# A state-space convolution block with a gated feed-forward on one core: ScalarE's table sets named in the program at four places of the front and once behind the last exponents

## The chip, the core and the metric

The kernel runs on one core of a Trainium2 chip, as one program. The metric is the device time of one execution in microseconds (us); lower is better. The core has TensorE (matrix products), VectorE and GpSimd (elementwise work), ScalarE (elementwise functions by table), and SyncE, which here only issues transfers. Each has a queue of its own that is worked off in order, and semaphores order one against another. In the views they are called PE (and PEld for its weight loads), DVE, POOL, ACT and SP.

## The reference

`x` is 2048 x 640, the state size is 128, the hidden size of the feed-forward 1728, all float32.

```python
mod = (silu(c) @ w_mod).reshape(1, 6, 1, 640)       # shift, scale, gate, twice
h = layernorm(x) * (1 + ca) + sa
x = x + ga * A(h)
h = layernorm(x) * (1 + cb) + sb
x = x + gb * B(h)

def A(u):                                           # a long convolution per channel
    dt = exp(log_dt)[:, None]
    logdA = dt * (A_re + 1j * A_im)
    P = exp(logdA[:, :, None] * arange(2048))
    K = einsum("dn,dnl,dn->dl", C, P, dt * B).real   # 640 filters of length 2048
    return irfft(rfft(u, 4096) * rfft(K, 4096))[:2048] + u * Dskip

def B(x):
    return (silu(x @ w1) * (x @ w3)) @ w2
```

## The kernel before

The program has three stretches: a front, a stretch in an order written out by hand (`ROUND`), and the feed-forward.

**The filters.** The powers `P` are built in polar form. `polar(cs, E)` (L237) works on the columns `cs` of the channels and turns `B` times `C` into a logarithm of its size (Square, then `Ln`, L256), an angle (`Abs`, `Arctan`, L262, and two `Sign`, L263 and L264), and the phases of the powers as integers (`thi`, `phi`). It is a generator: the program calls it once for channels 0 to 127 (`first`, on VectorE) and once for channels 128 to 639 (`rest`, whose first products are GpSimd's), in three steps each, with other work between the steps. Then, by blocks of 16 channels numbered 0 to 39, `exps` multiplies the logarithms by the powers' exponents on TensorE (`exp_fast`, L432, and `exp_slow`, L444, into the banks `pa` and `pq`) and takes the exponential on ScalarE (`fast`, `slow`: the tables `A`). `phases` forms the phase table `ph` on GpSimd, `absph`, `cosine` and `sine` take its absolute value, cosine and sine on ScalarE, and `real1`, `real2`, `imag1`, `imag2` (L497 to L508) multiply size by phase on VectorE into `E` and `A`. `kgen` (L521), `k1evac` and `k_stage1` (L539) make of these the filters and the first half of their Fourier transform; `k_out` copies it into `uk`.

**The input.** `ln1_load` brings tiles `x` of 128 rows, seven at a time, `ln1_norm` takes two of them through the layernorm (VectorE's statistics L377, GpSimd's power, VectorE's L381, ScalarE's Identity), and `u_stage1` (L406) does the first half of their transform: TensorE into `pu`, ScalarE's copy or VectorE's sums (L411, L412) into `u`, SyncE's store to `us` (L413).

**The modulation.** `mod_early`, `mod_shift`, `mod_gate` and `mod_cols` multiply silu(c) by `w_mod` on TensorE (L299, L310, L324, L333, L343) between the rest, with VectorE's copies `part` (L301). The silu of `c` itself is made of an exponential and a reciprocal.

**The front's loop** runs `tk` from 0 to 9. In the rounds `tk` = 2 and 6 it calls `exps` twice, for four blocks; after the second pair of round 2 it takes a step of `rest` (`next(rest)`), which holds `Ln`, `Arctan` and `Sign`; then come cosine and sine of the next block. ScalarE's instructions of the front are held in the program's order (`act`, L135, and `acopy`, L138, pass each to `keep_in_program_order`). VectorE's, TensorE's, GpSimd's and SyncE's are ordered by a scheduler there.

**ROUND** (10 rounds of 4 blocks) is one list of steps that all engines but SyncE follow: the rest of the filters, and by `stage2` (L570), `k_copy` (the copy `kc`), `products`, `sums`, `inverse1` (L612) and `z_store` the second half of the transforms, the product and the inverse, into `zs`. The tail of the convolution, `tk` from 41, has no exponents any more; at its first step the tables' room is given back (`tabs.close()`).

**The feed-forward** takes half of the tokens at a time and runs under L102, where a helper records every operation. It uses `Silu`, copies, casts and Identity of ScalarE.

**Table sets.** ScalarE's functions lie in tables, several functions to a set, and a set has to be loaded (`ACT_TABLE_LOAD`) before a function of it runs. The program before names none; the loads are put in when it is built, each ahead of the first function that the loaded set lacks.

Of the kernel before, what the change touches and what calls it, by code (L numbers as in the profile page):

```python
# [107 lines left out]
def tile_kernel(ctx: ExitStack, tc: tile.TileContext, a):  # L108
    nc = tc.nc
    V, S, G, PE = nc.vector, nc.scalar, nc.gpsimd, nc.tensor  # L110
# [22 lines left out]
    def act(*args, **kw):  # L133

        return tc.keep_in_program_order(S.activation(*args, **kw))  # L135

    def acopy(out, in_):
        return tc.keep_in_program_order(S.copy(out, in_))  # L138

    def ln_stats(pool, x):  # L140
        st = pool.tile([P, 2, 6], F32, name="st")
        V.bn_stats(st[:, 0, :], x[:, :320])
        V.bn_stats(st[:, 1, :], x[:, 320:])
        mv = pool.tile([P, 2], F32, name="mv")
        V.bn_aggr(mv, st)
        rs = pool.tile([P, 2], F32, name="rs")
        G.tensor_tensor(rs[:, 0:1], mv[:, 1:2], epst[:, 0:1], op=OP.add)
        G.tensor_tensor(rs[:, 1:2], rs[:, 0:1], epst[:, 1:2], op=OP.pow)
        return mv[:, 0:1], rs[:, 1:2]
# [87 lines left out]
    def polar(cs, E):  # L237

        are, aim, br, bi, cr, ci = (prm[:, i, cs] for i in range(6))
        ld, dtc, m, t, g_r, g_i = (v[:, cs] for v in (ldt, dt, m0, t3, gr, gi))  # L240
        k0, nk = cs.start // P, (cs.stop - cs.start) // P

        E.tensor_tensor(g_r, br, cr, op=OP.mult)
        E.tensor_tensor(m, bi, ci, op=OP.mult)
        E.tensor_tensor(g_r, g_r, m, op=OP.subtract)
        V.tensor_tensor(g_i, br, ci, op=OP.mult)
        V.tensor_tensor(t, bi, cr, op=OP.mult)
        V.tensor_tensor(g_i, g_i, t, op=OP.add)
        q, q2, ag, ai = br, bi, cr, ci
        act(q, g_r, AF.Square)  # L250
        act(q2, g_i, AF.Square)
        act(ag, g_r, AF.Abs)
        act(ai, g_i, AF.Abs)
        yield
        V.scalar_tensor_tensor(q, q, 1e-36, q2, op0=OP.max, op1=OP.add)
        act(q, q, AF.Ln)  # L256

        V.tensor_tensor(m, ag, ai, op=OP.subtract)
        V.scalar_tensor_tensor(t, ag, 1e-30, ai, op0=OP.max, op1=OP.add)
        V.reciprocal(q2, t)  # L260
        V.tensor_tensor(m, m, q2, op=OP.mult)
        act(m, m, AF.Arctan)  # L262
        act(ag, g_r, AF.Sign, scale=-1.0)  # L263
        act(ai, g_i, AF.Sign, scale=-1.0, bias=tiny)  # L264

        V.scalar_tensor_tensor(aim, aim, 0.25 / math.pi, dtc, op0=OP.mult, op1=OP.mult)
        magic = 12582912.0
        V.tensor_scalar(t, aim, magic, None, op0=OP.add)
        V.tensor_scalar(t, t, -magic, None, op0=OP.add)
        V.tensor_tensor(aim, aim, t, op=OP.subtract)  # L270
        V.tensor_scalar(thi[:, cs], aim, TURN, 2147483520.0, op0=OP.mult, op1=OP.min)
        yield

        nat = lambda v: v.rearrange("n (k p r j) -> n k r p j", k=nk, p=4, r=4)
        rows = lambda v: v[:, :nk * P].rearrange("n (k r p j) -> n k r p j", k=nk, p=4, r=4)
        for k in range(nk):
            E.tensor_tensor(rows(lt[:, 0])[:, k], nat(are)[:, k], nat(dtc)[:, k], op=OP.mult)
        for k in range(nk):
            V.tensor_tensor(rows(lt[:, 1])[:, k], nat(q)[:, k], nat(ld)[:, k], op=OP.add)
        for i, (hi, lo) in enumerate(((lah, lal), (lmh, lml))):  # L280
            pT = psS.tile([P, 2, 512], F32, name="pT", tag="AB"[i], bufs=1)
            for k in range(nk):
                PE.transpose(pT[:, 0, k * P:(k + 1) * P], lt[:, i, k * P:(k + 1) * P], ident)
            pv = pT[:, 0, :nk * P].rearrange("p (k n) -> p k n", k=nk)
            acopy(hi[:, k0:k0 + nk], pv)
            V.tensor_tensor(lo[:, k0:k0 + nk], pv, hi[:, k0:k0 + nk].bitcast(F32), op=OP.subtract)

        V.tensor_scalar(m, m, 0.5 / math.pi, 0.125, op0=OP.mult, op1=OP.add)
        V.tensor_tensor(m, m, ag, op=OP.mult)
        V.scalar_tensor_tensor(m, m, 0.25, ai, op0=OP.add, op1=OP.mult)  # L290
        V.tensor_scalar(phi[:, cs], m, TURN, 2147483520.0, op0=OP.mult, op1=OP.min)
# [132 lines left out]
    def exp_fast(steps):  # L424

        for s in steps:
            pA[s] = psS.tile([P, 2, 512], F32, name="pa", tag="AB"[s % 2] if not in_order[0] else "B", bufs=1)
        for w, st in ((lah, True), (lal, False)):
            for s in steps:
                ch, js, rows = exp_rows(s)  # L430
                for rr, r in rows:
                    keep(PE.matmul(pA[s][:, rr, :], w[r, ch, :], r2[r, js, :].rearrange("p j b -> p (j b)"),  # L432
                                   start=st, stop=not st, tile_position=(r.start, 0)))
# [13 lines left out]
    def fast(s):  # L447

        AA[s] = a_table()
        act(AA[s][:, :, 0:3:2, :], pA.pop(s).rearrange("p r (j h b) -> p (r j) h b", j=8, h=2), AF.Exp)  # L450
# [5 lines left out]
    def exps(s, between=()):  # L456

        steps = (s, s + 1)
        exp_fast(steps)
        for i in steps:  # L460
            fast(i)
        for fn in between:
            fn()
        exp_slow(steps)
        for i in steps:
            slow(i)
# [247 lines left out]
    def do(name, k):  # L714
# [4 lines left out]
        done.add((name, k))  # L719
        return (conv if name in conv else parts)[name](k)  # L720

    act(sc, cT, AF.Exp, scale=-1.0)
    act(dt, ldt, AF.Exp)
    V.tensor_scalar(sc, sc, 1.0, None, op0=OP.add)
# [22 lines left out]
        ln1_load(j)  # L747
    nc.sync.dma_start(prm[:, :, d1], prma[:, :, d1])
    mod_shift()
    exps(0)  # L750
    ln1_norm(0)
    exps(2)
# [21 lines left out]
    for tk in range(LAG):  # L774
        if tk == SPC + 1:
            mod_cols(4, wm[4])
            pre.close()
            fp = ssm.enter_context(tc.tile_pool(name="fp", bufs=2, side="right", reuse_waits="tile"))

        def transform_k():  # L780
            if 0 <= tk - 1:
                do("kg", tk - 1)
            if 0 <= tk - 2:
                do("pt", tk - 2)
                do("uk", tk - 2)

        do("PH", tk + 3)
        do("AB", tk + 2)
        if tk % EB == EB - 2:
            exps(tk + 2)  # L790
            transform_k()
            exps(tk + 4)
            done.update((n, k) for n in ("PA", "XA", "PQ", "XQ") for k in range(tk + 6))
            if tk == 2:
                next(rest)
        do("CO", tk + 2)
        do("SI", tk + 2)
        if tk % EB != EB - 2:
            transform_k()
        for n in ("E1", "E2", "A1", "A2"):  # L800
            do(n, tk)
        if 0 <= tk - 1:
            do("K", tk - 1)
        if tk < 6:
            for j in (2 * tk + 4, 2 * tk + 5):
                u_stage1(j)
            for j in (2 * tk + 7, 2 * tk + 8):
                if j < NT:
                    ln1_load(j)
            if tk + 3 < 8:  # L810
                ln1_norm(tk + 3)
        if tk == 0:
            next(rest)
        if tk == 3:
            next(rest, None)
            wm = []
        if 4 <= tk < 9:
            wm.append(w_load(w_room(2, tk % 2, WC, 2048), 1920 + (tk - 4) * WC))
        if 5 <= tk < 9:
            mod_cols(tk - 5, wm[tk - 5])  # L820
        if tk == 7:
            for i in range(4):
                u_load(0, i)
# [10 lines left out]
    for rnd in range(NS // EB):  # L834
        for word in ROUND:
            name, k = word[:2].rstrip("+-"), EB * rnd + int(word[len(word[:2].rstrip("+-")):])
# [9 lines left out]
    for tk in range(NS + 1, LAG + 8 * NDC + 2):  # L846
        do("st", tk)
        do("kc", tk)
        last = do("iv", tk - 1)
        do("zt", tk - 1)  # L850
        do("T", tk)
        do("Y", tk)
        if tk == NS + 1:
            tabs.close()
            xp = ctx.enter_context(tc.tile_pool(name="xp", bufs=2))
            idle = xp.tile([P, 512], F32R, name="idle", bufs=1)
            G.memset(idle.bitcast(F32), 0.0)
            for j in range(4):
                early[j] = (x_tile(), early[j][1], xp.tile([P, KD, 6], F32, name="st5", bufs=4))
        i = tk - 1 - LAG - 8 * NDC + 8  # L860
        if 0 <= i < 8:
            if i < 4:
                z_load(early[i][1], i, (3,), q=nc.gpsimd)
            for j in ((), (), (), (), (0,), (1,), (), (2, 3))[i]:
                x_part(j, last)
# [18 lines left out]
    V, S, G, PE = (InOrder(tc, e, (in_order,)) for e in (V, S, G, PE))  # L884
# [638 lines left out]
```

## Time and profile before

| | |
|---|---|
| three runs | 984.60, 984.23, 985.72 us, median 984.6 |
| profiled execution, span from first to last instruction | 984.1 us (the page gives no other time of it) |
| busy: TensorE | 918.2 us, 93% |
| VectorE | 700.8 us, 71% |
| ScalarE | 541.1 us, 55% |
| GpSimd | 265.3 us, 27% |
| mean granted clock of TensorE | 0.947 of full speed |

The page's second part cuts the span into 40 slices of 24.6 us and gives each engine's busy tenths in them, and the granted clock. The timeline lists an engine's instructions: start, us, engine, line, operation, output <- input, count, and in brackets the idle time before it with what ended it. Its start is that of the instruction, which may overlap the one before by some 0.1 us. The chain of waits follows the work that ended last back from the end, at each step to what released it. The view by groups adds up instructions of one line and one shape: busy us, mean ns of one, idle us before them and its releasers.

### The profile page before, as it was taken

The numbers are of one execution on the slowest core, as the hardware profiler recorded it, in microseconds if no ns is written. First come the engines' busy times: TensorE is split into PE (matmuls) and PEld (weight loads), VectorE is DVE, ScalarE is ACT, GpSimd is POOL, SyncE is SP. The second block draws the span as 40 slices with busy tenths as digits, with TensorE's granted clock in tenths as the row PEclk, the third lists the DMA queues.
The fourth block names the chain that finished last, engine by engine and source line by source line (L and its number), as shares of the span: only waits on it lengthen the run. The fifth ranks groups of instructions, "written<-read, shape, count | busy, mean of one in ns | idle before, by whom it ended". The sixth has DMA issues, their size and how long they took to land.

```text
span 984.1 us, 20582 instructions
## 1 busy us (share of the span) xinstructions
PE 918.2 (93%) x8214; PEld 687.2 (70%) x8214; DVE 700.8 (71%) x1253; ACT 541.1 (55%) x793; POOL 265.3 (27%) x274
## 2 busy tenths in 40 slices
PE   5898797989888898789999999999999999999998
PEld 2445354766666676567888888777888888888886
DVE  4598856888988886667766665568796766654575
ACT  3667665899999983246433332355753333323432
POOL 1453333444444440214422220111152222200000
PEclk9855767999999999989999999999999999999999
DMA  9463576554665587767212311896432221113443
GB/s 267 159 228 110 220 186 186 158 131 134 159 159 154 153 219 200 252 170 259 82 55 62 99 54 52 221 281 208 135 93 67 81 68 54 54 41 90 151 148 120
DMA packets 103572, 140.74 MB, mean 143 GB/s; under 512 B 20565, under 2 KB 62677, under 8 KB 103477
## 3 DMA queue, kind: packets, MB, share of 16 engines
q1 hardware_dynamic: 99668, 129.34, 45.5%
q0 software_dynamic: 2304, 7.74, 2.4%
q10 hardware_dynamic: 1504, 2.36, 0.9%
q8 instruction: 64, 1.05, 0.4%
q14 instruction: 32, 0.25, 0.1%
HBM read 107.94 MB, written 31.46 MB: 142 GB/s over the span
## 4 chain that ended last, share of the span: by engine, by line
PE 68%; ACT 15%; DVE 7%; DMA 4%; issue 3%; POOL 2%; SPq 1%; ACTq 0%; DVEq 0%; POOLq 0%
PE ps L102 52%; ACT cs L135 4%; ACT A L135 3%; ACT ph L135 3%; PE pa L432 2%; PE p L570 2%; ACT L135 2%; DMA zs<-zt 2%; PE pq L444 2%; PE pt L539 1%; PE pk L521 1%; PE pm L299 1%; DMA A<-zs 1%; PE pu L406 1%; PE pz L612 1%
## 5 line engine op out<-in xcount | busy, mean ns | idle before, releaser
L102 DVE TENSOR_TENSOR s<-ps,s 128x512 f32<-128x512 f32 x138 | 94.8, 687 | 79.8 <-PE ps L102 79.5
L472 POOL TENSOR_TENSOR ph<-thi,iota 128x1024 int32<-128x1024 int32 x40 | 85.4, 2135 | 175.1 <-DVE A L508 78.2
L102 DVE TENSOR_TENSOR gl<-rw,gh 128x640 fp32r<-128x640 f32 x87 | 78.1, 897 | 65.3 <-ACT gh L102 65.2
L102 ACT CAST gh<-rw 128x640 fp32r<-128x640 f32 x87 | 63.3, 727 | 103.9 <-PE ps L102 60.6
L570 PE MATMUL p<-uk,s 128*64 128x256 f32 x640 | 79.0, 389 | 13.3 <-PE pa L432 5.6
L102 PE MATMUL ps<-xA,gh 128*128 128x512 f32 x280 | 87.9, 392 | 0.4 <-ACT xA L102 0.4
L102 PE MATMUL ps<-gh,uh 128*128 128x512 f32 x224 | 87.5, 390 | 0.0
L102 PE MATMUL ps<-gl,uh 128*128 128x512 f32 x224 | 87.2, 389 | 0.0
L102 POOL TENSOR_TENSOR S<-rw 128x256 f32<-128x256 f32 x46 | 36.7, 799 | 174.0 <-DVE S0l L102 163.1
L102 PE MATMUL ps<-gh,ul 128*128 128x512 f32 x208 | 81.1, 390 | 0.0
L570 PEld LDWEIGHTS p<-uk,s 128*64 128x64 f32 x640 | 45.2, 138 | 38.5 <-PE pa L432 8.4
L102 PEld LDWEIGHTS ps<-xA,gh 128*128 128x128 f32 x280 | 52.1, 188 | 13.0 <-ACT xA L102 1.0
L102 PE MATMUL ps<-xA,gl 128*128 128x512 f32 x140 | 54.5, 390 | 0.0
L135 ACT ACTIVATE A<-pa 128x1024 f32<-128x1024 f32 x40 | 40.4, 1023 | 25.7 <-PE pa L432 24.3
L497 DVE TENSOR_TENSOR E<-A,cs 128x1024 f32<-128x1024 f32 x40 | 51.0, 1275 | 1.7 <-PE pk L521 1.7
L504 DVE TENSOR_TENSOR A<-A,ph 128x1024 f32<-128x1024 f32 x40 | 50.1, 1253 | 0.0
L612 PE MATMUL pz<-Y,i 64*128 64x128 f32 x640 | 45.2, 286 | 5.0 <-issue 3.1
L612 PEld LDWEIGHTS pz<-Y,i 64*128 64x128 f32 x640 | 39.1, 190 | 14.9 <-issue 11.4
L102 PEld LDWEIGHTS ps<-gl,uh 128*128 128x128 f32 x224 | 42.1, 188 | 8.9
L102 PEld LDWEIGHTS ps<-gh,uh 128*128 128x128 f32 x224 | 42.0, 188 | 8.8
L521 PE MATMUL pk<-E 128*32 128x64 f32 x1280 | 46.6, 232 | 1.2 <-DVE E L500 0.6
L539 PE MATMUL pt<-s,K 128*64 128x128 f32 x640 | 47.2, 291 | 0.5 <-ACT uk L138 0.5
(261 smaller groups left out, 2306.7 us busy)
## 6 DMA issues: line engine op xcount, KB each, us to landing
rw<-in_w_dram SPq DMA_DIRECT2D x52, 320.0 KB
us<-u SPq DMA_DIRECT2D x16, 640.0 KB
s<-in_s_dram SPq DMA_DIRECT2D x40, 256.0 KB
i<-in_i_dram SPq DMA_DIRECT2D x40, 256.0 KB
rw<-in_wg_dram SPq DMA_DIRECT2D x31, 320.0 KB
rw<-in_wu_dram SPq DMA_DIRECT2D x28, 320.0 KB
uk<-us SPq DMA_DIRECT2D x32, 256.0 KB
zs<-zt SPq DMA_DIRECT2D x32, 256.0 KB
```

The costliest lines, as they stand in the source:

```text
L102: ins = fn(*args, **kw)
L135: return tc.keep_in_program_order(S.activation(*args, **kw))
L299: PE.matmul(pm[g, :n], scb[:, k], w[:, k, :], start=(k < 4), stop=(k > 0), tile_position=(0, g.start))
L432: keep(PE.matmul(pA[s][:, rr, :], w[r, ch, :], r2[r, js, :].rearrange("p j b -> p (j b)"), start=st, stop=not st, tile_position=(r.start, 0)))
L444: keep(PE.matmul(pQ[s][:, rr, :256], w[r, ch, :], rv, start=(i == 0), stop=(i == 3), tile_position=(r.start, 0)))
L472: hold(G.tensor_tensor(p, bc(thi[:, sl], 2, NPH), bc(iota, 1, SD), op=OP.mult))
L497: keep(V.tensor_tensor(EC[s][:, :, 1:3, :], AA[s][:, :, 1:3, :], mid(cs[s]), op=OP.mult))
L504: keep(V.tensor_tensor(A[:, :, 1:3, :], A[:, :, 1:3, :], mid(ph[s]), op=OP.mult))
L521: keep(PE.matmul(pk[dq * 32:dq * 32 + 32, g, :], x[:, g * 4 + dq, 1, :], x[:, g * 4 + dq, 0:3:2, :], start=(st == 0), stop=(st == 1), tile ...
L539: keep(PE.matmul(pt[c * 64:c * 64 + 64, g, :], kk[:, g, :], s1[:, c, :], start=True, stop=True, tile_position=(0, c * 64)))
L570: keep(PE.matmul(p2[par * 64:par * 64 + 64, pi, c, :], s2[:, pi * 2 + par, c * 64:c * 64 + 64], uk[:, 0:kn + 1:kn, f, :], start=True, stop ...
L612: ins = keep(PE.matmul(pz[:, par, (g % 2) * 2 + pi, :], i1[r, pi, c, :], Y[r, pi, c, :], start=(c == 0), stop=(c == 1), tile_position=(par ...
```

## The change

A helper names a set, and is called at five places of the code. Since `polar` runs twice and one place is inside the loop's rounds 2 and 6, the calls come to seven.

- In `polar`, ahead of the arctangent, the set `trig_and_small`, which holds arctangent, sign, absolute value and sine.
- Ahead of the first exponentials (of `c` and `log_dt`), ahead of `exps(0)`, and ahead of `exps` in the rounds 2 and 6, the set `natural_log_exp_and_others`, which holds exponential and logarithm.
- At the first step of the convolution's tail, the set `silu_and_others`.

The named loads are held in the program's order, as ScalarE's other instructions of the front are. Where a function's set isn't there, loads are still put in when the program is built.

```diff
     def acopy(out, in_):
         return tc.keep_in_program_order(S.copy(out, in_))
+
+    def act_set(name):
+        tc.keep_in_program_order(S.preload_act_table_set(name))
...
         V.reciprocal(q2, t)
         V.tensor_tensor(m, m, q2, op=OP.mult)
+        act_set("trig_and_small")
         act(m, m, AF.Arctan)
...
+    act_set("natural_log_exp_and_others")
     act(sc, cT, AF.Exp, scale=-1.0)
     act(dt, ldt, AF.Exp)
...
     mod_shift()
+    act_set("natural_log_exp_and_others")
     exps(0)
     ln1_norm(0)
     exps(2)
...
         if tk % EB == EB - 2:
+            act_set("natural_log_exp_and_others")
             exps(tk + 2)
             transform_k()
             exps(tk + 4)
...
         if tk == NS + 1:
+            act_set("silu_and_others")
             tabs.close()
```

## The prediction

> **What bounds the kernel now.** I read the page first, then ScalarE's groups, then the chain of waits and the timelines around the places that the change touches.
>
> ```profile
> span 984.1 us, 20582 instructions
> PE   5898797989888898789999999999999999999998
> PEclk9855767999999999989999999999999999999999
> PE 68%; ACT 15%; DVE 7%; DMA 4%; issue 3%; POOL 2%; SPq 1%; ACTq 0%; DVEq 0%; POOLq 0%
> L135 ACT ACT_TABLE_LOAD x25 | 32.1, 1283 | 1.6 <-PEq L1512 1.2
> L102 ACT ACT_TABLE_LOAD x1 | 1.3, 1283 | 0.0
> ```
>
> The page gives a span and no other time of this execution: 984.1 us, 0.5 below the median of the three runs, 984.6 (984.23 to 985.72). I work on the span and move the median by the same amount. A measurement of this kernel can tell a difference of about 0.2%, 2 us, from none. TensorE carries 68% of the chain that ended last, and from slice 8 on (each is 24.6 us) it is nearly always busy at nearly full clock. The first seven slices are another kernel: TensorE less filled, and its granted clock down to half. ScalarE has 15% of the chain, and there are 26 loads of a table set, 1.283 us each. What a removed load is worth is read where it stands.
>
> **What the change does to the loads.** Placed by themselves before, each load stands where the function changes. The built program of after has 23 loads, all others in the same places of ScalarE's queue, and no load waits for a semaphore. Three go: the one ahead of the first polar part's logarithm (exponential and logarithm are now of one set), the one ahead of the logarithm of the second polar part, and the one ahead of the cosine behind the second polar part's signs (arctangent and sine are now of one set). The load for SiLU moves from the first SiLU to the tail of the convolution. ScalarE's other instructions keep their order. I cost these four one by one.
>
> First polar part, ScalarE's timeline:
>
> ```profile
> 10.05 1.28 ACT L135 ACT_TABLE_LOAD   x1
> 11.93 0.31 ACT L135 ACTIVATE uk<-uk 128x128 f32<-128x128 f32 x1 [0.60 <-DVE uk L255]
> 25.34 1.02 ACT L135 ACTIVATE A<-pa 128x1024 f32<-128x1024 f32 x1 [9.19 <-PE pa L432]
> ```
>
> The load at 10.05 ends at 11.33 and the logarithm starts at 11.93, because VectorE's L255 comes last, 0.60 later. Taking the load away moves nothing: cost zero, the cover is VectorE. The first exponents at 25.34 waited 9.19 for TensorE, so even without that cover the 1.28 would end in this wait.
>
> The trace of this place weighs a rule. The Trainium skill, "ScalarE: Activation LUTs", section "What ACT_TABLE_LOAD costs", counts 2.66 us for a switch, a load and a drain of 1.38. By the row the logarithm started 1.88 after the load did, so 2.66 does not fit here; by the rule the two loads of the second polar part would be worth 5.3 us on ScalarE, which VectorE's limit below would hold to the same sum.
>
> Second polar part, the chain of waits (start, us, what; the last row is a store of `u` that prices rival 3):
>
> ```profile
> 89.18 0.60 ACT A L135
> 89.80 1.28 ACT L135
> 91.09 0.63 ACT uk L135
> 91.74 1.28 ACT L135
> 93.57 1.23 ACT uk L135 x2
> 94.81 1.28 ACT L135
> 96.11 1.15 ACT cs L135
> 98.20 0.58 ACT u L138
> ...
> 117.00 5.44 DMA us<-u
> ```
>
> Here all three loads are on the chain. The first (89.80) and the third (94.81) go, the second stays. From the end of the last exponent, 89.18 + 0.60 = 89.78, to the logarithm at 91.09 are 1.31; from the load's start at 94.81 to the cosine at 96.11 are 1.30. ScalarE therefore stands 2.6 us earlier when it copies `u` at 98.20. I take 2.6.
>
> How much of this gets through is read from who waits behind it:
>
> ```profile
> 97.38 0.88 DVE L377 BATCH_NORM_STATS2 st<-x 128x6 f32<-128x320 f32 x2
> 98.83 2.17 PE L406 MATMUL pu<-x,misc 32*64 32x320 f32 x16 [3.73 <-ACT u L138]
> 100.25 0.82 DVE L411 TENSOR_TENSOR u<-pu,shift 128x640 f32<-128x640 f32 x1 [1.99 <-PE pu L406]
> 109.37 0.69 DVE L286 TENSOR_TENSOR lml<-pT,lmh 128x512 fp32r<-128x512 f32 x1 [0.48 <-ACT lmh L138]
> 119.23 1.73 ACT L135 ACTIVATE x<-x,rs 128x640 f32<-128x640 f32 x2 [5.74 <-DVE rs L381]
> 167.28 0.58 ACT L138 COPY kc<-p 128x512 f32<-128x512 f32 x1 [8.41 <-PE p L570]
> ```
>
> TensorE sat 3.73 for the copy and can take the whole 2.6. VectorE had waited 1.99 for TensorE at 100.25: that is all it can gain there, its own work ends at 98.26. It waits for ScalarE once more, 0.48 at 109.37, and that wait too is behind the removed loads. Together 2.47. At 119.23 ScalarE itself waits 5.74 for VectorE, so what passes this place is VectorE's gain, 2.47, not ScalarE's 2.6. Behind it the work goes on in chains of TensorE, VectorE and SyncE's stores to the first product copy at 167.28, where the order written out by hand begins. That order is the same in both programs, so a shift there reaches the end. This term: -2.5, between 0 and -2.6.
>
> SiLU's load, ScalarE's timeline at the new and at the old place:
>
> ```profile
> 383.89 0.90 ACT L694 COPY xm<-xe 128x128 f32<-128x128 f32 x4
> 386.10 0.58 ACT L138 COPY kc<-p 128x512 f32<-128x512 f32 x1 [1.31 <-PE p L570]
> 440.18 1.28 ACT L102 ACT_TABLE_LOAD   x1
> 441.91 0.60 ACT L102 ACTIVATE s<-ps 128x512 f32<-128x512 f32 x1 [0.45 <-PE ps L102]
> ```
>
> At the old place the first SiLU waited another 0.45 for TensorE, so the load was covered and removing it gains nothing. The new place is right ahead of the four small copies at 383.89. Queued behind it are these and the copy at 386.10, which waited 1.31 for TensorE; 1.28 fits into it, with 0.03 left. Cost 0, at worst 1.28 if TensorE comes that much earlier there.
>
> **The order of the other engines.** The named loads are seen by the scheduler, which sets TensorE, VectorE and SyncE anew up to about 140 us. The two built programs differ in it, and GpSimd's order does not. Three differences count.
>
> ```profile
> 18.61 0.79 PE L432 MATMUL pa<-r,lah 32*128 32x512 f32 x1
> 28.17 0.79 PE L432 MATMUL pa<-r,lal 32*128 32x512 f32 x2
> 48.08 0.61 PE L310 MATMUL pm<-misc,part 128*128 128x1 f32 x4 [1.10 <-DVE part L301]
> 43.00 0.34 SPq L368 DMA_DIRECT2D x<-in_x_dram  x1
> 55.19 0.33 SPq L413 DMA_DIRECT2D us<-u  x1
> 58.78 0.88 DVE L377 BATCH_NORM_STATS2 st<-x 128x6 f32<-128x320 f32 x2
> ```
>
> One: the first eight exponent products stood in five groups, from 18.61 to 28.17, each of 0.79 whether it held one product or two side by side on different rows of the array. In after they stand in three groups, ahead of most modulation products: at best 2 x 0.79 = 1.6 less. Two: the copy of `part` for the row at 48.08 stands ahead of a wait on GpSimd instead of behind it, at best 1.10. Both are TensorE time at a place where it is dense, yet the modulation chain that it also feeds ends where it did, so I take little: -0.5, between 0 and -2.7 (1.6 + 1.10). Three, a loss: SyncE now issues two stores of `u` ahead of the load of the eighth `x` tile, which was issued at 43.00 and now stands behind the store at 55.19. Its statistics ran at 58.78. I price it at 0, with a bound worked out as a rival below.
>
> Sum: 0 - 2.5 + 0 - 0.5 + 0 = -3.0. Forecast: 984.1 - 3.0 = 981.1 of span, 981.6 as a median.
>
> **The rivals.** (1) The clock, the slower side. The granted clock goes up and down in the front, by stages:
>
> ```profile
> 60.00:63.00 3.00, 3.00 (x48) 1.55 (x44) 2.81 (x5) 2.97 (x4) 0.51 (x2) 0.50 0.71 229
> 96.00:99.00 3.00, 0.17 (x4) 0.17 (x8) 2.25 (x6) 2.99 (x5) 2.84 (x2) 0.87 0.89 254
> 107.00:117.00 10.00, 8.13 (x210) 5.51 (x210) 9.52 (x19) 5.29 (x7) 2.95 (x2) 0.93 0.62 219
> 128.00:141.00 13.00, 12.89 (x118) 7.73 (x122) 5.04 (x9) 5.50 (x8) 4.77 (x3) 0.57 0.88 207
> ```
>
> (Columns: stage, its us, then busy of TensorE, weight loads, VectorE, ScalarE, GpSimd, then clock, DMA share, GB/s.) Moving matmuls by some us moves which of them run at which clock. If the stage from 107 to 117 lost its 0.93 and ran at 0.50, its 8.13 of TensorE would become 8.13 x 0.93 / 0.50 = 15.1, longer than the stage and than VectorE's 9.52: +5.1, and with the -3.0 a median of 986.7. It decides once TensorE's work there passes 10 us, that is below a clock of 0.76. For it: the clock is at half through most of the front, so the 0.93 is the exception. Against it: the same products stand there in the same density. Chance 0.2.
>
> (2) The clock the other way. The stage from 128 to 141 is TensorE's alone, 12.89 of 13.00 at 0.57. If a quarter of it came to full clock, 3.25 us would shrink to 1.85: -1.4 more, and for half of it -2.8. Median 978.8 to 980.2. Chance 0.15. The Trainium skill, "TensorE: Matmul & The Clock Gate", Part 1, says that a busy window of about 3.4 us lifts the clock and an idle one drops it. By it a TensorE wait cut from 3.73 to 1.1 at 98.83 would keep the full clock that the row at 96 shows going unused, and this rival would be likelier. The trace agrees only in part: at 60 to 63 TensorE is busy for 3.00 of 3.00 and stays at 0.50.
>
> (3) The late load of `x` eats the gain. The only transfer of this stretch that the chain shows whole took 5.44 (at 117.00, of twice the size). Issued behind the store, at 55.5, a load of at most 5.44 would land by 61.0 against statistics at 58.78: VectorE stalls by up to 2.2, ahead of the second polar part. Or VectorE's waits of 1.99 and 0.48 were filled by other late work. Either leaves between -0.3 and -1.9: no change to be told, some 984.0. Chance 0.2.
>
> (4) The names do nothing, and loads are put in a second time. The built order, with its 23, speaks against it; were it so, the time would stay 984.6. Chance under 0.01.
>
> **How the numbers follow.** Forecast, -2.0 to -4.0: 0.45. With rival 2, faster by over 0.2%: 0.60. Same, rival 3: 0.20. Slower, rival 1: 0.20. The likeliest case's own range is 980.6 to 982.6. For 8 in 10 I go down to 978.5, which takes in most of rival 2, and up to 986.5, which takes in rival 3 and most of rival 1's smaller sizes.
>
> **What would show it.** Right: 23 loads in ScalarE's group of loads; one load instead of three in ScalarE's run behind the second pair of exponents, and that run shorter by 2.6; VectorE's wait of 1.99 down to little; the first `kc` copy about 3.0 earlier than 167.28, and from there on the same distance to the end. The copy that stood at 386.10 shows no wait from the SiLU load beyond 0.1. Wrong: the first `kc` copy at 167 or later. If VectorE shows a new wait for a DMA of `x` near 59, it is rival 3; if the stage before 117 runs at half clock, rival 1. If the distance from the first `kc` copy to the end changes by over 1 us, the cause lies behind the front, and my assumption that a shift passes through is the step that failed.

## The result and the profile after

| | median | lowest to highest, executions | ratio to before, 95% interval |
|---|---|---|---|
| before | 986.08 us | 979.73 to 989.15, 16 | |
| changed kernel | 978.98 us | 973.97 to 983.21, 16 | 0.9926 (0.9906 to 0.9946) |

The change makes the kernel 7.1 us faster, where the forecast said 3.0. A fact that goes with it: executions of one and the same program lie some 9 us apart (973.97 to 983.21). The profiled execution of the changed kernel took 973.97 with a span of 972.2, its fastest; a second profile of the same program has a span of 980.5. What one pair of profiles shows is therefore not yet the effect of the change.

The page of the changed kernel (its first profile), and ScalarE's groups of loads:

```profile
span 972.2 us, 20575 instructions
PE   5898788899898889799999999999999999999998
PEclk8755789999999999999999999999999999999999
PE 69%; ACT 14%; DVE 7%; DMA 4%; POOL 3%; issue 2%; ACTq 0%; SPq 0%; POOLq 0%; DVEq 0%
```

```profile
L135 ACT ACT_TABLE_LOAD x16 | 20.5, 1283 | 0.3
L141 ACT ACT_TABLE_LOAD x7 | 9.0, 1283 | 1.3 <-PEq L1520 1.2
```

There are 23 loads (16 + 7), as announced, and the picture of the engines is the old one: a front of seven slices with the clock down to half, then TensorE. ScalarE's timeline at the places of the prediction (start, us, engine, line, operation, count, idle before and releaser):

```profile
16.93 1.02 ACT L135 ACTIVATE A<-pa 128x1024 f32<-128x1024 f32 x1 [1.72 <-PE pa L436]
28.23 1.09 ACT L135 ACTIVATE A<-pq 128x512 f32<-128x512 f32 x2 [9.36 <-PE pq L448]
...
83.41 0.60 ACT L135 ACTIVATE A<-pq 128x512 f32<-128x512 f32 x1 [0.32 <-PE pq L448]
83.90 0.62 ACT L135 ACTIVATE uk<-uk 128x512 f32<-128x512 f32 x1
84.54 1.28 ACT L141 ACT_TABLE_LOAD   x1
85.83 1.15 ACT L135 ACTIVATE uk<-uk 128x512 f32<-128x512 f32 x2
86.89 0.71 ACT L135 ACTIVATE uk<-uk,tiny 128x512 f32<-128x512 f32 x1
87.50 1.13 ACT L135 ACTIVATE cs<-cs,hp 128x1024 f32<-128x1024 f32 x1
88.54 1.04 ACT L135 ACTIVATE ph<-ph 128x1024 f32<-128x1024 int32 x1
89.49 0.67 ACT L138 COPY u<-pu 128x640 f32<-128x640 f32 x1
...
103.02 0.58 ACT L138 CAST lmh<-pT 128x512 fp32r<-128x512 f32 x1 [2.94 <-PE pT L287]
112.90 0.92 ACT L135 ACTIVATE x<-x,rs 128x640 f32<-128x640 f32 x1 [5.14 <-DVE rs L385]
158.32 0.58 ACT L138 COPY kc<-p 128x512 f32<-128x512 f32 x1 [7.59 <-PE p L574]
```

(The rows at 16.93 and 112.90 show the first of two instructions each.) Behind the second pair of exponents stands one load, at 84.54; the logarithm (83.90) stands right ahead of it, and the cosine (87.50) follows the signs without a load. The first exponents, at 25.34 before, are at 16.93, and the exponents of `pq` behind them now wait 9.36 for TensorE. Before, these waited little:

```profile
31.10 1.09 ACT L135 ACTIVATE A<-pq 128x512 f32<-128x512 f32 x2 [1.06 <-PE pq L444]
```

So of the 8.4 us that the first exponents come sooner, 2.9 are left at the next ones. The first `kc` copy is 8.96 earlier than 167.28, three times what was announced.

VectorE behind the removed loads:

```profile
90.54 0.82 DVE L416 TENSOR_TENSOR u<-pu,shift 128x640 f32<-128x640 f32 x1
103.64 0.69 DVE L290 TENSOR_TENSOR lml<-pT,lmh 128x512 fp32r<-128x512 f32 x1 [1.55 <-ACT lmh L138]
```

Its wait of 1.99 at the `u` sum is gone, but the one ahead of `lml` went from 0.48 to 1.55, because TensorE's second `pT` comes later: ScalarE's copy `lmh` (103.02) waits 2.94 for it, where it waited 1.14. TensorE's two groups of `pT`, before and in the changed kernel:

```profile
105.88 1.11 PE L283 MATMUL pT<-ident,lt 128*128 128x128 f32 x4
107.72 1.00 PE L283 MATMUL pT<-ident,lt 128*128 128x128 f32 x4
```

```profile
98.38 1.09 PE L287 MATMUL pT<-ident,lt 128*128 128x128 f32 x4 [0.88 <-DVE u L416]
101.87 1.12 PE L287 MATMUL pT<-ident,lt 128*128 128x128 f32 x4
```

They stand 1.84 apart before and 3.49 in the changed kernel, because the new order puts 62 products of `pk` and two of `pt` between them where before there are 24 of `pk`. This is the order's doing and not the loads': `loads_only`, with the loads gone, does not have it (24 products between the groups), and `first_trig`, with one load back, does. `order_only` (16 products) does not have this part of the new order either.

### The profile page after: what moved, and what is told of

It is laid out like the page before. It is cut to its first block, busy times and chain, and to the rows that moved or that the text cites. A ratio compares the mean times of both kernels' runs of the same rounds, so it can differ in the third digit from the quotient of the medians.

```text
span 972.2 us, 20575 instructions
## 1 busy us (share of the span) xinstructions
PE 906.3 (93%) x8214; PEld 683.5 (70%) x8214; DVE 701.9 (72%) x1253; ACT 537.3 (55%) x790; POOL 266.2 (27%) x274
## 4 chain that ended last, share of the span: by engine, by line
PE 69%; ACT 14%; DVE 7%; DMA 4%; POOL 3%; issue 2%; ACTq 0%; SPq 0%; POOLq 0%; DVEq 0%
PE ps L102 56%; ACT cs L135 3%; ACT A L135 3%; PE p L574 3%; ACT ph L135 3%; DMA zs<-zt 2%; PE pq L448 2%; ACT L135 2%; PE pt L543 1%; PE pa L436 1%; POOL ph L476 1%; PE pm L303 1%; PE pk L525 1%; PE pz L616 1%; ACT zt L138 1%
## 5 line engine op out<-in xcount | busy, mean ns | idle before, releaser
L508 DVE TENSOR_TENSOR A<-A,ph 128x1024 f32<-128x1024 f32 x40 | 50.2, 1254 | 0.0
L102 ACT ACTIVATE s<-ps 128x512 f32<-128x512 f32 (+1 forms) x33 | 19.6, 595 | 52.6 <-PE ps L102 52.6
```

The lines of the kernel that those rows point to most:

```text
L102: ins = fn(*args, **kw)
L508: keep(V.tensor_tensor(A[:, :, 1:3, :], A[:, :, 1:3, :], mid(ph[s]), op=OP.mult))
```

## Experiments: the parts of the change

Kernels that ran on the same chip share the runs of the kernel before there: its median is 984.97 for `silu_only`, `loads_only`, `order_only` and `after_again`, 987.31 for `first_trig`, `before_warm`, `after_warm` and `after_fill`, and 986.11 for the other four. Each ratio is to these.

**The SiLU load alone.**

```diff
         if tk == NS + 1:
+            act_set("silu_and_others")
             tabs.close()
```

> The kernel before with the SiLU set named at the first step of the convolution's tail, nothing else; the orders of all engines are those of before. Both theories: no difference, within 1 us of before; the load stands right ahead of the four small copies near 384 and the next `kc` copy waits for TensorE all the same. A rival: it costs or gives over 1.3 us, since TensorE's tail hangs on the copy behind it.

Measured: 984.75, ratio 0.9996 (0.9979 to 1.0014). ScalarE's timeline at the new place:

```profile
384.46 1.28 ACT L141 ACT_TABLE_LOAD   x1
385.75 0.90 ACT L697 COPY xm<-xe 128x128 f32<-128x128 f32 x4
386.56 0.57 ACT L138 COPY kc<-p 128x512 f32<-128x512 f32 x1
```

The copy starts without a wait; the load has taken the place of its 1.31 on TensorE. This part is worth nothing that can be measured, as forecast.

**The two loads of the second polar part alone**, in nearly the old order (up to 104 us the engines' orders are those of before).

```diff
         V.tensor_tensor(m, m, q2, op=OP.mult)
+        if E is G:
+            act_set("trig_and_small")
         act(m, m, AF.Arctan)
...
         if tk % EB == EB - 2:
+            act_set("natural_log_exp_and_others")
             exps(tk + 2)
```

> The kernel before with sets named ahead of `exps` in the loop and, in the second polar part only, ahead of its arctangent. The two loads of the second polar part are gone (24 loads in the built program); all engines keep the order of before up to that place. Theory A (the loads are worth what they take on the chain, the new order of the front the rest): -2.5 us against before; the copies of `u` at 59.80 and the last exponent at 89.18 stay within 1 us, the first `kc` copy comes at 164.8. Theory B (the loads carry the whole gain of 7): -5 to -7 us.

Measured: 984.17, ratio 0.9995 (0.9978 to 1.0012). By itself the removal of the two loads cannot be seen in the time; at most 2.2 us lie within the interval, so the 2.5 of theory A is not there, and theory B's 5 to 7 still less. Its profile:

```profile
94.05 0.67 ACT L138 COPY u<-pu 128x640 f32<-128x640 f32 x1
101.55 0.69 ACT L138 COPY u<-pu 128x640 f32<-128x640 f32 x1 [1.64 <-DMA us<-u]
106.56 0.58 ACT L138 CAST lmh<-pT 128x512 fp32r<-128x512 f32 x1 [1.26 <-PE pT L288]
117.64 1.73 ACT L135 ACTIVATE x<-x,rs 128x640 f32<-128x640 f32 x2 [6.35 <-DVE rs L386]
```

The copy of `u` that is at 98.11 in the profile before comes 4.06 sooner here. Not all of that is the loads': from the copy of `u` ahead of the loads to this one it takes 21.59 here and 22.57 in `loads_fill` below, where the same two loads are gone, against 25.42 before. Then a wait of 1.64 for a store of `u` appears (101.55), and at the last `x` of the front, 119.23 before, 1.59 is left.

**The order alone**: the names that make the scheduler set the new order, with the second polar part's three loads kept.

```diff
         V.tensor_tensor(m, m, q2, op=OP.mult)
+        if E is V:
+            act_set("trig_and_small")
         act(m, m, AF.Arctan)
...
+    act_set("natural_log_exp_and_others")
     act(sc, cT, AF.Exp, scale=-1.0)
```

> The kernel before with sets named ahead of the first exponentials and, in the first polar part only, ahead of its arctangent. The built program has the order of after on TensorE, VectorE and SyncE up to about 95 us, but the three loads of the second polar part (25 loads). Theory A: -4 to -5 us against before; first exponents near 17, the copy of `u` that stood at 59.80 near 52, the last exponent of the second four near 83.5, the two extra loads then push the first `kc` copy to 161. Theory B: 0, the first `kc` copy near 167.

Measured: 982.22, ratio 0.9976 (0.9960 to 0.9993). The order, priced at 0.5, gives 2.8 (0.7 to 3.9 by the interval) with all three loads still there; theory A's 4 to 5 is not reached, theory B's 0 is out.

**The changed kernel again, on this chip.**

> The changed kernel once more, as the yardstick on this chip: 979, -7 us against before. Its profile tells which part of the 11.9 us between the two profiled spans comes back: by the medians 7; the first `kc` copy near 159 if the front's gain is that of the first profile.

Measured: 976.86, ratio 0.9932 (0.9910 to 0.9953). By the medians the loads alone are 0.8, the order alone 2.8, and both with SiLU 8.1 us below the before of the same chip. By the ratios, which carry the intervals, the parts are 0.5, 2.4 and 0.4 (SiLU) and the whole is 6.7: 3.4 more than the sum. The four intervals together leave some 3.6 (an estimate: their half widths, 1.7, 1.6, 1.7 and 2.1, taken as independent), so that the parts fall short of the whole is likely and not shown. Nor are they exact parts: behind 98 to 104 us the single programs are ordered otherwise than the changed kernel, as the `pT` groups show.

**The changed kernel with one of the second polar part's loads back.**

```diff
         if tk % EB == EB - 2:
-            act_set("natural_log_exp_and_others")
             exps(tk + 2)
```

(The calls ahead of `exps(0)` and at the tail are out too.)

> The changed kernel with the table set ahead of the second polar's exponentials taken out again (and the one behind the last exponents, which made no difference by itself): the order of the changed kernel, two of the three loads of the second polar merged by the trig_and_small call, 24 loads. Theory P (the gain is path alone: order plus loads, 1.3 us for each load taken off the second polar): about 1.3 us above the changed kernel, so 5.0 to 5.8 below the kernel before. Theory C (what goes beyond 3.0 us comes from the TensorE clock, which is granted in steps of 3.415 us on a grid that is not tied to the program, so that small shifts change which steps are granted in full): no simple share; anything from 2.4 (the order alone) to 7 below, and a spread of several us among its executions.

Measured: 980.41, ratio 0.9923 (0.9894 to 0.9952), 6.9 below before: level with the changed kernel (0.9926 and 0.9932 in its two measurements). In its profile the stretch between the copies of `u` that held the loads is 24.26 long against 22.84 in the changed kernel's, so the load costs there what it should, 1.4. It is not to be seen in the total; with six executions the interval is 2.9 us wide to each side and could not have shown it, so this run does not decide between theories P and C.

## Experiments: the clock

Why should the whole be more than its parts, and why do executions of one program differ? The granted clock of TensorE, read in windows of 3.41 us, gives a lead. The changed kernel's first profile (stage, its us, busy of TensorE, weight loads, VectorE, ScalarE, GpSimd, clock, DMA share, GB/s):

```profile
107.21:110.63 3.42, 2.82 (x94) 2.07 (x95) 3.42 (x8) 0.55 (x1) 2.29 (x2) 1.00 1.06 415
110.63:114.05 3.42, 0.89 (x18) 0.33 (x24) 2.56 (x6) 1.15 (x2) 1.69 (x2) 1.00 0.54 210
114.05:117.46 3.41, 2.71 (x42) 1.12 (x35) 3.41 (x7) 3.38 (x4) 2.11 (x1) 0.51 0.00 0
117.46:120.88 3.42, 3.42 (x28) 1.46 (x25) 3.42 (x5) 3.40 (x5) 2.09 (x2) 0.50 0.39 159
120.88:124.29 3.41, 3.41 (x22) 0.82 (x20) 1.16 (x2) 2.09 (x3) 2.02 (x2) 0.50 0.60 229
124.29:127.70 3.41, 3.20 (x65) 2.60 (x66) 1.29 (x3) 1.08 (x2) 0.92 (x1) 0.99 0.49 130
...
137.95:141.37 3.42, 0.83 (x26) 0.65 (x25) 3.42 (x7) 3.39 (x5) 1.99 (x1) 1.00 1.24 194
141.37:144.78 3.41, 3.08 (x18) 1.75 (x18) 3.36 (x2) 0.86 (x1) 2.20 (x2) 0.50 1.16 214
144.78:148.19 3.41, 3.41 (x89) 2.40 (x86) 1.95 (x5) 3.10 (x4) 1.04 (x1) 1.00 1.07 337
```

And before, the same stretch of work:

```profile
115.30:118.71 3.41, 1.79 (x31) 1.06 (x24) 2.88 (x5) 0.00 (x0) 2.01 (x3) 1.00 1.05 397
118.71:122.12 3.41, 1.91 (x24) 0.77 (x24) 3.08 (x6) 2.85 (x4) 0.73 (x2) 0.50 0.38 159
122.12:125.54 3.42, 2.84 (x38) 1.36 (x34) 3.42 (x5) 3.42 (x5) 3.34 (x2) 0.50 0.00 0
...
135.78:139.20 3.42, 3.42 (x25) 1.57 (x22) 3.25 (x6) 1.53 (x3) 0.03 (x1) 0.50 1.23 207
139.20:142.62 3.42, 3.20 (x60) 2.13 (x58) 0.56 (x1) 3.16 (x5) 2.92 (x2) 1.00 0.62 99
```

Cut at the right phase, every window has one clock, half or full. By the clock's record in the traces the switches lie on a grid of 3.413 us over the whole span in all fourteen profiles (the expectations below say 3.415), but the grid is not tied to the program: in the changed kernel's two profiles it lies at 1.45 and 3.19 us after the start (modulo 3.413), before at 2.65. A window without much work (110.63, 0.89 busy) is followed by one at half. A full one of small products is too: at 117.46 TensorE is busy all the time and the next window still has 0.50. The Trainium skill, "TensorE: Matmul & The Clock Gate", Part 1, has a free-running window of 3413 ns and two clocks, and with that the traces agree; that the clock follows how busy TensorE was, they do not show.

From here there are two theories, P (path alone) and C (clock), as the expectations have them.

**Dense work at the start**, where TensorE is idle until 9.5 us, in both kernels:

```diff
+    dense = lml.rearrange("p k n -> p (k n)")[:, :512]
+    G.memset(dense.bitcast(F32), 0.0)
+    pd = psS.tile([P, 2, 512], F32, name="pd", tag="Z", bufs=1)
+
+    def dense_first(n):
+        for _ in range(n):
+            tc.keep_in_program_order(PE.matmul(pd[:, 0], dense[:, :P], dense, start=True, stop=True))
...
+    dense_first(12)
     act(sc, cT, AF.Exp, scale=-1.0)
```

> The kernel before with 12 dense 128x512 fp32r matmuls on a zeroed tile ahead of TensorE's first own one (TensorE is idle until 9.5 us; nothing else moves). Theory C: the clock steps that begin before about 9.5 us are granted in full, so the first matmuls run at 0.6 instead of 1.0 us a group until 10 to 13 us; the first evacuation of the exponents comes 0 to 1.5 us sooner and the end 0 to 3 us sooner. Theory P (the clock at the start plays no part): 0, within 0.5 us.

> The changed kernel with the same 12 dense matmuls at its start. Theory C: fewer of the late executions (the two profiles of the changed kernel differ by 8.3 us in span, the faster one with full clock at 15.1 to 18.5 us and the slower one at half there), median 0 to 3 us below the changed kernel, spread smaller. Theory P: 0, within 0.5 us.

Measured: `before_warm` 985.99, 0.9984 (0.9968 to 0.9999); `after_warm` 980.10, 0.9932 (0.9907 to 0.9958). The first is 1.3 below before by the medians (0.1 to 3.2 by the interval), the second stays level with the changed kernel. In both profiles the clock falls to half at 9.8 and 9.7 us, before the front's own products can use it. This test decided little.

**Dense work at the last `x` of the front**, ten products into unused columns, and a control with a 32x32 corner of the array, in the same order of all instructions:

```diff
         one = j % 2 == 0
+        for _ in range(10 if j == 14 else 0):
+            tc.keep_in_program_order(PE.matmul(pu[0][:, 0, 320:448], ident, ident, start=True, stop=True))
```

In the control that line reads:

```diff
-            tc.keep_in_program_order(PE.matmul(pu[0][:, 0, 320:448], ident, ident, start=True, stop=True))
+            tc.keep_in_program_order(PE.matmul(pu[0][:NA, 0, 320:448], ident[:NA, :NA], ident[:NA], start=True, stop=True,
+                                               tile_position=(0, 0)))
```

> The changed kernel with 10 dense 128x128 float32 matmuls into unused columns of the accumulator at the place where TensorE waits 2.5 us for the last x of the front (near 111 us). They take 2.0 us at full clock and 3.7 at half. Theory C: the steps of the clock around 111 to 117 us are granted in full more often, the half-clock stretch behind it (10 us in one profile of the changed kernel, 7 in the other, 20 in the kernel before) gets shorter, and the end comes 1 to 4 us sooner. Theory P: no gain; 0 to 1.5 us later, as far as the ten reach beyond the wait.

> The kernel with ten dense matmuls at the last x, each cut to a 32x32 corner of the array: the same order of every instruction, the same streamed columns, a sixteenth of the array at work. Theory C (the share of the array at work in a step of 3.415 us decides the clock of the next step): the gain of the dense ones goes, the time is back at the changed kernel's, about 7 us below the kernel before, with its spread of 6 to 9 us. Rival O (the order that the ten bring, not their work): as fast as with the dense ones, 11 to 12 us below the kernel before.

> The changed kernel with the ten dense matmuls once more, beside its control. Theory C: 10 to 12 us below the kernel before, spread of about 3 us, 3 to 5 us below the control. Rival O: level with the control.

Measured: `after_fill` 975.77, 0.9889 (0.9871 to 0.9907), executions 974.76 to 977.64; on another chip `after_fill_again` 975.76, 0.9894 (0.9871 to 0.9917), and the control `after_small` 979.64, 0.9927 (0.9906 to 0.9948). The control is back at the changed kernel's level. The ten useless products take TensorE 2.5 to 3.0 us in the profiles (2.50 at full clock in `before_fill`, where the expectation said 2.0). By the medians they make the kernel 3.9 us faster than the same ten on a sixteenth of the array (some 1 to 6, an estimate from the six executions of each); that speaks for their work and against their order, and so for C. Its forecast of a spread of about 3 us held on the first chip and not on the second, where the dense ten's executions go from 972.41 to 978.88. And the profiles do not show the work acting: in the control's one profile the clock behind the ten goes the same way as with the dense ones, from the last `x` to the first `kc` copy it takes 43.98 against 44.53, and the whole lead of the dense ten's profile is there before the ten run (the copy of `u` at 65.58 against 71.17, in the table below). That the dense executions were lucky in their start is a rival that no run excludes. By its medians the changed kernel with the dense ten is the fastest version of this study.

**The same ten in the kernel before, and with the loads alone.**

> The kernel before with the same ten dense matmuls at the same place (TensorE waits 3.1 us there). Theory C: its half-clock stretch behind 119 us (20.5 us in three profiles of this front) is cut, so it gains more than the changed kernel did, 4 to 9 us, and the changed kernel with the ten is then only about 3 us faster than this one, which is what the path alone gave in the prediction. Rival (the changed kernel's whole 7 us lie on the path): this one gains no more than the 4 us that the changed kernel gained, and the difference of the two stays at 7.

> The kernel before with the second polar's two loads merged away (no other order before 104 us) and the ten dense matmuls. Theory C: with the clock steadied the loads' 2.5 us show: 2 to 3 us below the kernel before with the ten, where without the ten nothing was seen (0.5 us, within the interval). Rival (the loads are not on the path): level with the kernel before with the ten.

Measured: `before_fill` 984.93, 0.9984 (0.9966 to 1.0002); `loads_fill` 986.47, 1.0006 (0.9990 to 1.0023). Here C fails twice. Before gains 1.2 instead of 4 to 9, the two kernels with the ten are 9.2 apart and not 3, and the loads do not come out. Both outcomes are what the rivals said, that the changed kernel's gain lies on its path and that the loads do not (9.2 is even more than their 7). The profile of `before_fill` has the stretch at half cut from 20.5 to 10.2 us, and the first `kc` copy 3.29 earlier:

```profile
119.73 1.73 ACT L135 ACTIVATE x<-x,rs 128x640 f32<-128x640 f32 x2 [5.75 <-DVE rs L381]
163.99 0.58 ACT L138 COPY kc<-p 128x512 f32<-128x512 f32 x1 [6.72 <-PE p L572]
```

But from there to the end it takes 819.2 us where the kernel before takes 816.8.

## Where the time went, by stages

The fourteen profiles, by starts in ScalarE's timelines, in us: the copies of `u` on both sides of the second polar part, the last `x` of the front, the first `kc` copy; and the span.

| profile | `u` ahead | `u` behind | last `x` | first `kc` | span |
|---|---|---|---|---|---|
| before | 72.69 | 98.11 | 119.23 | 167.28 | 984.1 |
| silu_only | 72.94 | 98.36 | 119.61 | 167.74 | 983.6 |
| before_warm | 73.13 | 98.41 | 119.55 | 167.60 | 984.2 |
| before_fill | 73.06 | 98.49 | 119.73 | 163.99 | 983.2 |
| loads_only | 72.46 | 94.05 | 117.64 | 162.48 | 979.2 |
| loads_fill | 73.24 | 95.81 | 118.31 | 168.52 | 985.1 |
| order_only | 64.63 | 90.31 | 112.81 | 162.84 | 979.0 |
| first_trig | 68.90 | 93.16 | 116.11 | 164.71 | 981.5 |
| after | 66.65 | 89.49 | 112.90 | 158.32 | 972.2 |
| after_again | 71.35 | 94.19 | 117.74 | 164.26 | 980.5 |
| after_warm | 70.53 | 93.35 | 116.13 | 160.80 | 977.9 |
| after_small | 71.17 | 94.00 | 116.80 | 160.78 | 977.3 |
| after_fill | 68.07 | 90.89 | 113.81 | 157.76 | 972.9 |
| after_fill_again | 65.58 | 88.41 | 111.43 | 155.96 | 972.8 |

I take the mean of the first three as before and of `after`, `after_again` and `after_warm` as after. Up to `u` ahead: 72.92 to 69.51, -3.4. From there to `u` behind: 25.37 to 22.83, -2.5. To the last `x`: 21.17 to 23.25, +2.1. To the first `kc`: 48.08 to 45.54, -2.5. To the end: 816.43 to 815.74, -0.7. Together -7.1, which is also the difference of the medians; by single profiles each of these but the second may be some us off. (In the new order alone, with all three loads, the second stretch is 25.68, so the two loads are worth 2.85 there.)

The first term is the new order, and it is not one number. In the six profiles with the old order that `u` stands between 72.46 and 73.24, wherever the grid lay. In the eight with the new order it lies between 64.63 and 71.35. One place where its executions part is the wait of the first `pq` exponents for TensorE. The changed kernel with the dense ten (second time):

```profile
24.25 1.08 ACT L135 ACTIVATE A<-pq 128x512 f32<-128x512 f32 x2 [5.10 <-PE pq L450]
```

```profile
16.15 0.61 PE L314 MATMUL pm<-misc,part 128*128 128x1 f32 x4
```

And its control (both programs follow the changed kernel's order until shortly ahead of the ten, near 110 us):

```profile
29.77 1.09 ACT L135 ACTIVATE A<-pq 128x512 f32<-128x512 f32 x2 [9.69 <-PE pq L451]
```

```profile
16.38 1.01 PE L314 MATMUL pm<-misc,part 128*128 128x1 f32 x4
```

The same four products took 0.61 in one execution and 1.01 in the other, full clock and half, and the wait was 5.10 or 9.69. The old order's six profiles all have 1.01 or 1.02 there. (The granted clock's record cannot tell: up to the first switch it reads 1.00 in either case.) So in the new order the beginning of the front hangs on TensorE's clock. The three profiles with 0.61 there (`order_only`, `after`, `after_fill_again`) win 6.3 to 8.3 us up to that `u`, the five with 1.01 win 1.6 to 4.9. The grid fits this: of the eight profiles with the new order the three with 0.61 have it at 1.45, 1.83 and 1.99 us (modulo 3.413), so that a window begins at 15.10 to 15.64, near the exponents' first products, and the five with 1.01 have it at 0.19, 0.22, 0.74, 2.91 and 3.19. That the place of the grid decides is still argued; it wasn't set on purpose in any run.

## Why the prediction was right or wrong

The direction, the number of loads and the range were right. The forecast of 981.6 was 2.6 us above the median of the changed kernel, and against the before of the same runs the gain is 7.1 where the sum said 3.0. That 978.98 lies within the range, 0.5 above its lower end, is in part luck: the range went down to 978.5 for rival 2, half a stage at full clock, and by the stages most of what came beyond the sum came from the order's term, outside that term's bounds.

**First polar load, 0: right.** The first exponents wait for TensorE still, 1.72 at 16.93.

**Second polar part, -2.5: right at its place, wrong behind it.** ScalarE's 2.6 are there: the stretch between the two copies of `u` is 25.37 before and 22.83 after, within 0.02 in every profile with both loads gone and the new order. The failing step is "what passes this place is VectorE's gain, 2.47". VectorE's 1.99 went, but its other wait, of 0.48, did not go; it grew by 1.07, since the new order puts more of TensorE's products between the two `pT` groups, which the three differences of the prediction do not have. By the last `x` the changed kernel has given back 2.1. Not all of this need be the loads' doing: the order alone, with all loads, takes 22.50 for that stretch in its one profile, against 21.17 before. Alone, in the old order, the removal is worth nothing that can be measured.

**SiLU, 0: right**, by its own run (within 2 us) and its row.

**The order, -0.5 between 0 and -2.7: the term that was mis-sized.** It measured -3.4 in the mean of three profiles up to the copy of `u`, and -2.8 alone in the total (0.7 to 3.9 by the interval), against a bound of -2.7. I counted the products' own TensorE time, 1.6 and 1.10, in a stage that I took to end where it did. The rows would have allowed the other question: the first exponents waited 9.19 for TensorE at 25.34, and the new order put their products ahead of most of the modulation, so they could come 8 us sooner. They did, but the next exponents then waited 9.36 for TensorE, and only 2.9 of it went on in this profile (28.23 against 31.10); one has to follow the shift to the next wait as well.

**The late load of `x` (rival 3): did not come.** VectorE shows no new wait for a transfer near its statistics.

**The clock (rivals 1 and 2).** Rival 2, half of the stage from 128 to 141 at full clock for 2.8 less, may have come true beside the sum: half clock lasts until 124 in the changed kernel's first profile against 139 before, and the stretch from the last `x` to `kc` is 2.5 shorter in the mean. That the one makes the other is argued; `order_only` has half clock until 132 and takes 50.0 for that stretch, longer than before. Rival 1's stage before 117 kept its full clock in that profile. What I had not seen is that the clock's windows lie anew in each execution.

**"The same distance to the end."** It held to 0.3 us only from the first `kc` copy to the 33rd (218.8 to 219.1 in all profiles). From the first `kc` to the end the profiles range from 813.9 to 819.2, whatever the kernel: my sign that "the cause lies behind the front" over 1 us was too fine for one profile.

**What stays open.** Why the loads, 2.5 at their place, do not show at all in the old order: over half is given back by the last `x` in both profiles (4.06 to 1.59 and 2.30 to 0.92 sooner than in the profile before), and the stretch behind it is 44.8 in one and 50.2 in the other. Their order behind 104 us differs from before's too (VectorE's from 114.57 on), and no run parts that from the loads. And how the dense ten gain 4 us in the changed kernel but hardly any before, if it is not the luck of few executions.

## What to carry to other kernels

When an edit changes what a scheduler sees, cost the new order by who waits first for the moved work (here ScalarE's 9.19 for TensorE), then by the next wait that takes it back (9.36), not by the busy time that the moved instructions save. Where two parts of a change do not seem to add up, ask first whether their intervals could show it, and compare several profiles of the same program stage by stage before explaining a difference: here two executions of one program differ by 4.7 us at the same copy. Useless dense work in an idle gap may be worth its time, and has to be tried in each kernel: here it was 3.9 us in one and 1.2, within the interval of none, in the other.

## What the runs showed of the hardware

TensorE's granted clock is either half or full, in windows of 3.413 us that run free of the program, in all fourteen profiles; the same products take 1.01 or 0.61 us. Up to the first switch the record reads full clock in either case. The executions of one program spread over 9 us of 980; in the new order the profiles with 0.61 at the start come 6.3 to 8.3 us sooner to the copy of `u` than before, the others 1.6 to 4.9. A window in which TensorE is busy for 3.42 of 3.42 us with products on a part of the array can be followed by half clock, and with ten dense products in place of ten on a sixteenth of the array the kernel's median was 3.9 us lower, by six executions of each. Two of ScalarE's table loads of 1.283 us, taken away with the rest in the same order, made the stretch around them 2.85 us shorter (25.68 to 22.83).
